# A state of 64 columns a head, and the inter part in 64 by 64 tiles, in a linear attention fused with a highway layer

## The chip, the core and the metric

The kernel runs on one core of a Trainium2 chip. The metric is the device time of one execution in microseconds. TensorE (PE) multiplies, VectorE (DVE), ScalarE (ACT) and GpSimd (POOL) do the elementwise work, and SyncE (SP) issues the transfers.

## What is computed

There are 4 sequences, 8 heads, 768 positions and 64 values a head. Attention is linear with a decay `lam` per head, done in blocks of 64 positions, with a 64 by 64 state carried from block to block:

```python
intra = np.einsum('bhic,bhjc->bhij', qb, kb) * Dmask[None]
intra = np.einsum('bhij,bhjd->bhid', intra, vb)
inter = np.einsum('bhid,bhde->bhie', qb * lam_pow[None], kv_state)
out[:, :, sl] = intra + inter
kv_state = lam_block[None, :, None, None] * kv_state + np.einsum('bhsd,bhse->bhde', kb_dec, vb)
...
x = np.ascontiguousarray(attn_out.transpose(0, 2, 1, 3)).reshape(B * S, H * D)
H = np.maximum(x @ w_h, 0.0)
T = 1.0 / (1.0 + np.exp(-(x @ w_t + b_t)))
return (T * H + (1.0 - T) * x).astype(np.float32)
```

The second part, a highway layer, takes the 3072 rows of 512 values that the attention gives.

## The kernel before

The work is cut into 12 chunks `n` of 256 positions, three to a sequence, and each chunk into two halves `b` of 128. The decay is moved into powers: `v` is weighed by `pow_v` when it is cast, the attention's result by `pow_o` when it leaves PSUM, so that the state only sums. The state is kept in one PSUM bank, `kv`, for the four pairs of heads `hp`; `e` is the head in its pair, and stands for the lower or upper 64 partitions.

For a chunk the kernel loads q, k and v, each in two transfers of 256 KB (`Lq`, `Lk`, `Lv`), casts them (`CQ`, `CK`, `CV`), turns q and k on PE (`RQF`, `RKF`, full 128 by 128 transposes, or `RQ`, `RK`, by 64 rows), evacuates them (`EQ`, `EK`, `FQ`, `FK`), multiplies scores (`S`, or `SA` and `SB` with state tiles between) and masks them on DVE (`M`), adds to the state (`U`) and copies the state out (`KE`, tile `ss`). The result `o` is a PSUM bank per half: `I` multiplies the inter part, `A` adds the intra part, and `D` brings it to `xT`. In `ss` a pair of heads is a 128 by 128 matrix, whose two blocks off the diagonal are zero, so `I` is one 128 by 128 matmul for a pair and a half:

```python
for hp in range(NP):
    T.matmul(get("o", n, b)[:, hp, :], lhsT=buf("ss", n, b)[:, hp, :], rhs=q_cols(n, slice(0, 128), hp, b),
             start=hp == 0, stop=False, skip_group_check=True)
```

The highway layer is done for each half of 128 rows, all 512 columns at a time. `TX` or `TXB` turns `xT` back to rows, which `XC` copies to `xs`; `BP` writes the bias into a bank, on which `F` with w=1 adds the four t matmuls, and `G` is the sigmoid; `F` with w=0 makes h in another bank. Then `H` takes max(h, 0) - x to `y` (DVE), `X` multiplies by the gate (POOL, sometimes DVE), `Y` adds x (POOL) and `ST` stores 512 KB. The last chunk goes another way in narrower pieces (`P`, `R`, `HX`, `YL`). The weights come in four transfers of 512 KB (`W`, 256 rows of w_h or w_t each) and are cast by `WC`. `Z` multiplies a blank tile to no use.

The order is written out by hand: `PLAN` is a list of such tokens, with the engine behind `@` and the PSUM banks behind `=`, and every engine works off its own part of the list in that order. All loads and stores go through one queue, SP's, and `UNDER_WAY` lets it issue a transfer only when the one eight places earlier has landed. Input buffers are rings of four chunks.

Of the kernel before, what the change touches and what calls it, by code (L numbers as in the profile page):

```python
# [21 lines left out]
WC.1.1.1@DVE Z.3=0 KE.1.0@ACT D.0.0@DVE Lv.2.1 WC.1.0.1@ACT WC.1.0.0@POOL M.1.0.1 U.1.1 TXB.0.0=0 BP.0.0.2@ACT=3
M.1.1.1 I.1=64 KE.1.1@ACT D.0.1@DVE F.0.0.1.2 Lk.3.1 WC.0.1.1@POOL WC.0.1.0@ACT M.1.0.0 BP.0.1.2@ACT=1 TXB.0.1=5 A.1.1
G.0.0.2 A.1.0 Lk.3.0 WC.0.0.1@DVE F.0.1.1.2 WC.0.0.0@ACT D.1.1@DVE XC.0.2.1@ACT Lq.3.1 F.0.1.0.2=2 D.1.0@DVE
XC.0.2.0@ACT Lq.3.0 G.0.1.2@S BP.1.1.2@DVE=4 TXB.1.1=5 F.0.0.0.2=0 H.0.1.2 Lk.5.1 CQ.2.2@ACT XC.1.2.1@DVE F.1.1.1.2
X.0.1.2@POOL H.0.0.2 Lv.3.1 CK.2.2@ACT BP.1.0.2@DVE=6 RQF.2=5 Lv.3.0 G.1.1.2@S Y.0.1.2@POOL TXB.1.0=1 X.0.0.2@DVE
RKF.2=2 XC.1.2.0@ACT F.1.1.0.2=0 EQ.2.1@DVE Lq.5.1 EK.2.0@ACT EK.2.1@DVE CV.2.2@POOL EQ.2.0@ACT S.2.1=14 Lk.4.1
H.1.1.2 F.1.0.1.2 M.2.0.1 Lk.5.0 CK.3.2@ACT S.2.0=25 M.2.1.1 X.1.1.2@POOL U.2.0 Lq.4.1 F.1.0.0.2=1 M.2.1.0 KE.2.0@ACT
Lq.4.0 CQ.3.2@ACT Y.0.0.2@POOL M.2.0.0 I.2=45 H.1.0.2 RKF.3=3 Lq.5.0 G.1.0.2@S A.2.1 Y.1.1.2@POOL EK.3.0@DVE
EK.3.1@ACT A.2.0 RQF.3=2 Lk.4.0 D.2.1@DVE X.1.0.2@POOL EQ.3.0@ACT D.2.0@DVE TXB.2.1=3 Lv.4.1 F.2.1.0.2=0  # L30
BP.2.1.2@ACT=1 EQ.3.1@DVE Lv.4.0 CV.3.2@POOL BP.2.0.2@DVE=6 XC.2.2.1@ACT TXB.2.0=2 F.2.1.1.2 H.2.1.2 XC.2.2.0@ACT
Lv.5.1 S.3.1=32 G.2.1.2@S S.3.0=54 Lq.6.1 Y.1.0.2@POOL M.3.0.1 U.3.0 CK.5.2@ACT F.2.0.0.2=0 Lq.6.0 M.3.1.0
X.2.1.2@POOL KE.3.0@ACT M.3.0.0 F.2.0.1.2 Lk.6.1 H.2.0.2 Lv.5.0 RKF.5=3 CQ.4.2@POOL G.2.0.2@S M.3.1.1 I.3=45 U.3.1
Lk.6.0 CK.4.2@ACT EK.5.1@DVE A.3.0 CQ.5.2@POOL A.3.1 EK.5.0@DVE RQF.4=2 D.3.0@DVE Lk.7.0 KE.3.1@ACT RKF.4=3
Y.2.1.2@POOL D.3.1@DVE BP.3.0.2@ACT=1 RQF.5=0 Lv.6.1 EQ.4.0@DVE EK.4.1@ACT TXB.3.0=6 TXB.3.1=4 EQ.5.0@DVE CV.4.2@POOL
F.3.1.0.2=5 EQ.5.1@ACT XC.3.2.0@DVE EK.4.0@DVE XC.3.2.1@ACT EQ.4.1@DVE S.5.0=60 H.3.1.2 F.3.0.1.2 CQ.6.2@ACT
X.2.0.2@POOL M.5.1.0 Lv.8.1 SA.4=3 M.5.0.0 Lv.6.0 S.4.1=42 BP.3.1.2@ACT=5 F.3.0.0.2=0 M.4.1.0 Y.2.0.2@POOL Lq.7.0
KE.4.0@ACT M.4.1.1 G.3.0.2@S F.3.1.1.2 Lk.8.1 CV.5.2@POOL H.3.0.2 CK.6.2@ACT SB.4=6 M.4.0.1 S.5.1=32 I.4=10 M.4.0.0
KE.4.1@ACT RKF.6=4 G.3.1.2@S M.5.0.1 X.3.0.2@POOL Lv.9.1 U.5.0 EK.6.0@ACT A.4.0 M.5.1.1 A.4.1 Lq.7.1 KE.5.0@ACT
RQF.6=6 X.3.1.2@POOL D.4.0@DVE EK.6.1@ACT Lq.8.0 I.5=32 EQ.6.1@DVE BP.4.0.2@ACT=5 TXB.4.0=1 Lq.9.1 D.4.1@DVE A.5.1  # L40
CV.6.2@POOL A.5.0 Lv.7.0 XC.4.2.0@DVE F.4.0.0.2=4 D.5.0@DVE Lk.7.1 D.5.1@DVE TXB.4.1=1 BP.5.0.2@ACT=0 Lk.8.0 TXB.5.0=3
F.4.0.1.2 Y.3.1.2@POOL H.4.0.2 XC.4.2.1@ACT Lv.7.1 XC.5.2.0@ACT BP.5.1.2@DVE=2 TXB.5.1=1 Lk.10.0 F.5.0.0.2=4 G.4.0.2@S
Y.3.0.2@POOL EQ.6.0@DVE Lv.8.0 XC.5.2.1@ACT BP.4.1.2@DVE=5 SA.6=3 Lq.9.0 X.4.0.2@POOL S.6.1=61 H.5.0.2 KE.6.0@ACT
F.5.0.1.2 Lk.9.1 M.6.1.0 CQ.7.2@POOL F.4.1.1.2 M.6.0.1 Lk.9.0 G.5.0.2 M.6.1.1 F.5.1.0.2=3 Y.4.0.2@POOL Lq.8.1
CK.7.2@ACT X.5.0.2@DVE F.4.1.0.2=6 H.5.1.2 G.4.1.2 CK.8.2@POOL Lk.11.0 RKF.7=1 Lk.10.1 H.4.1.2 SB.6=4 CV.7.2@POOL
EK.7.1@ACT RQF.7=0 EK.7.0@DVE KE.6.1@ACT M.6.0.0 I.6=13 RKF.8=6 EQ.7.1@ACT X.4.1.2@DVE A.6.0 EQ.7.0@ACT CV.8.2@POOL
EK.8.0@DVE A.6.1 Lv.11.0 EK.8.1@ACT S.7.1=45 D.6.1@DVE SA.7=0 Lq.11.1 CQ.9.2@ACT F.5.1.1.2 M.7.0.1 Lv.9.0 M.7.1.1
BP.6.1.2@ACT=3 TXB.6.1=6 Y.4.1.2@POOL F.6.1.0.2=4 Lv.10.0 XC.6.2.1@ACT M.7.1.0 Lv.10.1 KE.7.0@ACT F.6.1.1.2 D.6.0@DVE
CQ.8.2@POOL G.5.1.2@S Lq.10.0 H.6.1.2 CK.9.2@ACT TXB.6.0=5 Lq.11.0 SB.7=6 X.5.1.2@POOL XC.6.2.0@DVE RQF.8=0 M.7.0.0
KE.7.1@ACT I.7=51 Lv.11.1 EQ.8.1@DVE G.6.1.2@S Y.5.0.2@POOL RQF.9=6 CK.10.2@ACT A.7.1 Lq.10.1 EQ.9.1@DVE A.7.0  # L50
S.8.1=24 X.6.1.2@POOL Lk.11.1 D.7.1@DVE F.6.0.0.2=3 EQ.9.0@ACT EQ.8.0@ACT M.8.1.1 ST.3 CV.9.2@POOL F.7.1.0.2=6
BP.7.1.2@ACT=1 H.6.0.2 ST.2 D.7.0@DVE SA.8=0 BP.6.0.2@ACT=3 SB.8=4 M.8.1.0 F.7.1.1.2 KE.8.0@ACT ST.4 CV.10.2@POOL
BP.7.0.2@ACT=5 M.8.0.0 RKF.9=0 ST.0 G.7.1.2@S M.8.0.1 F.7.0.0.2=4 EK.9.0@ACT ST.1 EK.9.1@DVE TX.7.2=21 CQ.11.2@POOL
SA.9=0 XC.7.2.0@DVE F.7.0.1.2 XC.7.2.1@DVE KE.9.0@ACT Y.5.1.2@POOL M.9.1.0 CQ.10.2@ACT I.8=21 H.7.1.2 SB.9=0
CK.11.2@POOL ST.5 G.7.0.2@S H.7.0.2 A.8.1 A.8.0 KE.9.1@ACT RQF.11=6 D.8.1@DVE CV.11.2@POOL S.9.1=54 EQ.11.0@ACT
# [15 lines left out]

UNDER_WAY = 8

BUFS = dict(kf=4, qf=4, vf=4, kb=3, qb=2, vs=3, kT=2, qT=3, m=8, ss=4, xT=3, xs=3, y=6, ob=6, g=3)


@with_exitstack
def kernel(
# [13 lines left out]
    C = 128  # L92
# [404 lines left out]
```

## Time and profile before

| | |
|---|---|
| median of 3 runs | 105.09 us (105.09 to 105.13) |
| the profiled execution | 104.68 us, of which the span is 102.9 us |
| busy: PE, DVE, POOL, ACT | 92.4, 87.2, 78.9, 76.8 us |
| moved by transfers | 27.52 MB, mean 267 GB/s |
| mean granted clock of PE | 0.995 |

Times in the profile are microseconds from the start of the span. A group's row gives line, engine, operation, tiles, forms and count, then its busy time and the mean of one in ns, then the idle time ahead of it and what ended it. A row of the chain gives start, duration, engine, tile and line; a row of the table by stretch gives the stretch and its length, then the busy time of PE, weight loads, DVE, ACT and POOL with counts, the clock, the share of the transfer engines and GB/s. Busy times of PE hold pipelined latency, so the mean of one matmul is not its cost.

### The profile page before, as it was taken

What the parts mean: (1) busy time and instruction counts of PE and PEld (TensorE: products, weight loads), DVE (VectorE), ACT (ScalarE), POOL (GpSimd) and SP (SyncE); (2) the same over time, 40 slices, a digit from 0 to 9 for tenths busy, and PEclk for the clock granted to TensorE, in tenths of its full rate; (3) what the DMA queues carried; (4) which work ended last, traced back from release to release, by engine and by line L of the source; (5) the groups of instructions that cost most, each with busy time, mean ns of one, the idle gap of its engine ahead of it and who ended that gap; (6) DMA issues with size and microseconds to landing.
All of it is one profiled execution on the core that took longest, in us unless ns stands there. A gap on an engine that the chain in (4) does not pass through costs nothing.

```text
span 102.9 us, 4082 instructions
## 1 busy us (share of the span) xinstructions
PE 92.4 (90%) x1706; PEld 57.4 (56%) x1725; DVE 87.2 (85%) x164; ACT 76.8 (75%) x132; POOL 78.9 (77%) x78
## 2 busy tenths in 40 slices
PE   5997998899898999999999989999999899999900
PEld 1443565556376668458654865846745746555400
DVE  4237989599898799999999799797997999999960
ACT  3599974999968878989587679995996675584600
POOL 6704452406999999999989995999999969689540
PEclk9999999999999999999999999999999999999997
DMA  1999999999999999999999999999991361415243
GB/s 19 272 312 317 292 369 387 354 307 287 297 322 331 329 283 293 292 294 310 331 310 300 314 310 317 323 335 395 403 380 70 128 255 37 156 48 202 111 164 138
DMA packets 33479, 27.52 MB, mean 267 GB/s; under 512 B 1460, under 2 KB 26420, under 8 KB 33461
## 3 DMA queue, kind: packets, MB, share of 16 engines
q1 hardware_dynamic: 33456, 27.27, 87.4%
q8 instruction: 13, 0.21, 0.9%
q14 instruction: 6, 0.04, 0.1%
q10 hardware_dynamic: 4, 0.00, 0.0%
HBM read 20.97 MB, written 6.29 MB: 265 GB/s over the span
## 4 chain that ended last, share of the span: by engine, by line
PE 61%; ACT 10%; SPq 9%; DMA 8%; issue 4%; DVE 3%; POOLq 1%; POOL 1%; ACTq 0%
PE bt L386 17%; PE bh L386 16%; SPq L194 9%; DMA w_f<-in_moe_w_t_dram 8%; PE bs L273 5%; PE bo L343 5%; PE bo L334 4%; PE kv L278 3%; PE bktr L244 3%; PE bx L362 3%; PE bqtr L244 3%; ACT kT L113 2%; ACT w_b L113 2%; ACT g L404 2%; ACT xs L113 1%
## 5 line engine op out<-in xcount | busy, mean ns | idle before, releaser
L315 DVE TENSOR_TENSOR m<-bs,tri 128x512 bf16<-128x512 f32 x48 | 30.8, 682 | 0.9 <-PE bs L273 0.9
L386 PEld LDWEIGHTS <-xT 128*128 128x128 bf16 x200 | 17.1, 98 | 16.9 <-issue 0.4
L408 POOL TENSOR_TENSOR y<-g,y 128x512 bf16<-128x512 f32 x17 | 19.7, 1161 | 8.1 <-DVE y L399 6.0
L412 POOL TENSOR_TENSOR ob<-y,xs 128x512 f32<-128x512 bf16 x21 | 24.1, 1159 | 0.6 <-DVE y L408 0.3
L386 PE MATMUL bh<-w_b,xT 128*128 128x512 bf16 (+2 forms) x94 | 23.8, 362 | 0.6 <-issue 0.2
L232 POOL TENSOR_TENSOR vs<-vf,pow_v 128x1024 bf16<-128x1024 f32 (+1 forms) x12 | 21.9, 1835 | 3.0 <-DMA vf<-in_v_dram 2.9
L386 PE MATMUL bt<-w_b,xT 128*128 128x512 bf16 x89 | 23.3, 380 | 0.9 <-issue 0.8
L349 DVE TENSOR_TENSOR xT<-bo,pow_o 128x512 bf16<-128x512 f32 x24 | 15.9, 683 | 0.4 <-PE bo L343 0.3
L399 DVE SCALAR_TENSOR_TENSOR y<-bh,xs 128x512 bf16<-128x512 f32 x23 | 15.6, 685 | 0.6 <-PE bh L386 0.2
L404 ACT ACTIVATE g<-bt 128x512 f32<-128x512 f32 x18 | 10.8, 598 | 4.3 <-PE bt L386 4.2
L113 ACT ACTIVATE ss<-kv 128x512 bf16<-128x512 f32 x19 | 11.3, 593 | 3.5 <-PE kv L278 3.4
L273 PE MATMUL bs<-qT,kT 64*64 64x128 bf16 x384 | 11.7, 220 | 0.5 <-ACT qT L113 0.3
L113 ACT ACTIVATE bt<-b_bc 128x512 f32<-128x512 f32 x18 | 10.7, 601 | 1.6 <-DVE xT L349 1.0
L273 PEld LDWEIGHTS <-kT 64*64 64x64 bf16 x384 | 8.1, 106 | 3.2 <-DVE kT L115 1.1
L113 ACT ACTIVATE kb<-kf 128x1024 bf16<-128x1024 f32 x9 | 9.5, 1059 | 0.2 <-DMA kf<-in_k_dram 0.2
L278 PE MATMUL kv<-vs,kb 64*64 64x64 bf16 x320 | 8.9, 195 | 0.7 <-issue 0.7
L278 PEld LDWEIGHTS <-kb 64*64 64x64 bf16 x320 | 6.9, 109 | 3.9 <-issue 2.9
L113 ACT ACTIVATE xs<-bx 128x512 bf16<-128x512 bf16 x13 | 7.5, 593 | 1.2 <-PE bx L362 0.9
L343 PE MATMUL bo<-m,vs 64*64 64x128 bf16 x384 | 8.2, 218 | 0.2 <-DVE m L315 0.2
L113 ACT ACTIVATE kT<-bktr 128x512 bf16<-128x512 bf16 x10 | 6.0, 597 | 2.8 <-DVE kT L115 1.5
L115 POOL CAST qb<-qf 128x1024 bf16<-128x1024 f32 (+1 forms) x6 | 5.8, 972 | 2.8 <-DMA qf<-in_q_dram 2.8
L115 DVE COPY kT<-bktr 128x512 bf16<-128x512 bf16 x12 | 5.0, 421 | 3.4 <-PE bktr L244 2.1
(72 smaller groups left out, 135.2 us busy)
## 6 DMA issues: line engine op xcount, KB each, us to landing
qf<-in_q_dram SPq DMA_DIRECT2D x24, 256.0 KB, 5.1
kf<-in_k_dram SPq DMA_DIRECT2D x24, 256.0 KB, 5.4
vf<-in_v_dram SPq DMA_DIRECT2D x24, 256.0 KB, 5.4
out_dram<-ob SPq DMA_DIRECT2D x11, 512.0 KB, 4.9
w_f<-in_moe_w_t_dram SPq DMA_DIRECT2D x2, 512.0 KB, 6.8
w_f<-in_moe_w_h_dram SPq DMA_DIRECT2D x2, 512.0 KB, 9.5
out_dram<-ob SPq DMA_DIRECT2D x1, 256.0 KB, 2.0
out_dram<-ob SPq DMA_DIRECT2D x2, 64.0 KB, 1.6
```

The source lines that it names most:

```text
L113: A.activation(dst, src, AF.Copy)
L232: ENG[eng].tensor_tensor(buf("vs", n)[:, hs], in0=buf("vf", n)[:, hs].rearrange("p h (j d) -> p h j d", j=J), in1=pow_v[:, n % NST, hs, :, ...
L273: T.matmul(get("s", n, e, hp // 2)[half(b), hp % 2, j, :], lhsT=buf("kT", n)[half(e), hp, j, half(b)], rhs=q_cols(n, half(e), hp, b), star ...
L278: T.matmul(kv[half(e), hp, half(e)], lhsT=buf("kb", n)[half(b), j, 2 * hp + e, :], rhs=buf("vs", n)[half(b), 2 * hp + e, j, :], start=firs ...
L315: V.tensor_tensor(buf("m", n, e, u), in0=get("s", n, e, u), in1=tri[:, None].to_broadcast([128, 2, J, C]), op=ALU.mult)
L343: T.matmul(get("o", n, b)[half(e), hp, :], lhsT=buf("vs", n)[half(b), 2 * hp + e, j, :], rhs=buf("m", n, e, hp // 2)[half(b), hp % 2, j, : ...
L349: V.tensor_tensor(cut(buf("xT", n)[:, :, b * C:(b + 1) * C]), in0=get("o", n, b).rearrange("e k (j p) -> e k p j", j=Q), in1=cut(pow_o[:, ...
L386: T.matmul(t, lhsT=buf("xT", n)[:, j, b * C:(b + 1) * C], rhs=w_b[w][:, j, z], start=(j == 0 and not w), stop=(j == KC - 1), skip_group_ch ...
L399: V.scalar_tensor_tensor(buf("y", n, b)[:, z], in0=get("h", n, b, p), scalar=0.0, in1=buf("xs", n)[:, b, z], op0=ALU.max, op1=ALU.subtract)
L404: A.activation(buf("g", n, b)[:, cols(p)] if to == "S" else t, t, AF.Sigmoid)
L408: ENG[eng].tensor_tensor(y, in0=buf("g", n, b)[:, cols(p)] if eng == "POOL" else get("t", n, b, p), in1=y, op=ALU.mult)
L412: ENG[eng].tensor_tensor(buf("ob", n)[:, b, z], in0=buf("y", n, b)[:, z], in1=buf("xs", n)[:, b, z], op=ALU.add)
```

## The change

The state bank now holds 64 columns for a pair: head `e` of a pair lies in partition half `e`, and both heads share the columns. `ss` is half as wide. Two heads can no longer be one 128 by 128 matmul, so `I` multiplies 64 by 64 tiles, eight for a half of the chunk instead of four matmuls. Tiles that read the upper and the lower partitions may not write one bank together, so each of two groups pairs the lower head of one half `b` with the upper head of the other. For odd pairs of heads the result goes to the opposite partition half; `pow_o`, the weights' rows, `XC` and the transposes of `xT` (with a matrix `swap`) follow that order. Between the groups stands `RD`, a read of one column of the result's bank, for which the second group waits:

```diff
-    def inter(n, bk):
-        o_banks(n, bk)
-        for b in range(2):
-            if n % NST or b:
-                for hp in range(NP):
-                    T.matmul(get("o", n, b)[:, hp, :], lhsT=buf("ss", n, b)[:, hp, :], rhs=q_cols(n, slice(0, 128), hp, b),
-                             start=hp == 0, stop=False, skip_group_check=True)
-                begun.update((n, b, e) for e in range(2))
+    def inter(n, straight, bk):
+        if not straight:
+            o_banks(n, bk)
+        for u in range(2):
+            for e in range(2):
+                b = e if straight else 1 - e
+                if n % NST == 0 and b == 0:
+                    continue
+                for hp in (2 * u, 2 * u + 1):
+                    z = e ^ (hp % 2)
+                    i = T.matmul(get("o", n, b)[half(z), hp, :], lhsT=buf("ss", n, b)[half(e), hp, :], rhs=q_cols(n, half(e), hp, b),
+                                 start=o_first(n, b, z), stop=False, skip_group_check=True)
+                    if ("seen", n) in made:
+                        tc.add_manual_dep(i.ins, made.pop(("seen", n)), ...)
+    def order_rows(n, eng):
+        b = int(n % NST == 0)
+        made["seen", n] = read(eng, seen[half(b)], get("o", n, b)[half(b), 3, 0:1]).ins.name
```

The highway layer of chunks 0 and 1 (`COLUMNS`) is done by column halves: a block `F` takes both row halves and 256 columns, and the weights come by column halves in twelve transfers of 128 or 256 KB. `W.w.g.i` is matrix, column half and piece:

```diff
-    def load_w(w, g):
-        move(out=w_f[w][:, 2 * g:2 * g + 2],
-                          in_=(moe_w_h, moe_w_t)[w][256 * g:256 * g + 256].rearrange("(kc p) m -> p kc m", p=128))
+    def load_w(w, g, i):
+        z = slice(256 * g, 256 * g + 256)
+        w_in = (moe_w_h, moe_w_t)[w].rearrange("(j s p) m -> p j s m", s=4, p=64)[:, :, :, z]
+        if i == 0:
+            move(out=w_f[w][:, 0::2, z], in_=(moe_w_h, moe_w_t)[w].rearrange("(j s) m -> s j m", s=256)[0:128, :, z])
+        else:
+            move(out=w_f[w][half(i - 1), 1::2, z], in_=w_in[:, :, 4 - i])
```

Six units of 128 rows (2.1, 7.0, 9.1, 10.1, 10.0 and 11.0) take the gate another way, without `xs`, `X` and `Y`: `HP` is max(h, 0) times the gate, `RP` is (gate - 1) times x straight from the transposes' bank, and `Q` subtracts the second from the first:

```diff
+    def upper(n, b):
+        V.scalar_tensor_tensor(buf("ob", n)[:, b], in0=get("h", n, b, 2), scalar=0.0, in1=buf("g", n, b), op0=ALU.max, op1=ALU.mult)
+    def lower(n, b):
+        V.scalar_tensor_tensor(buf("r", n, b), in0=buf("g", n, b), scalar=1.0, in1=get("x", n, 2, b).rearrange("p k f -> p (k f)"),
+                               op0=ALU.subtract, op1=ALU.mult)
+    def merge(n, b, eng):
+        o = buf("ob", n)[:, b]
+        ENG[eng].tensor_tensor(o, in0=o, in1=buf("r", n, b), op=ALU.subtract)
```

`PLAN` is written anew. The 21 blank matmuls of `Z` become 16, the bias is written by ACT 23 times of 24, chunks 7 to 11 turn q and k by 64 rows instead of chunk 10 alone, and chunks 3, 4, 5 and 8 turn `xT` by 64 rows instead of 7, 8 and 9.

On SP, at the program's start, the loads stood like this before; `w_f1` is w_t, `w_f0` is w_h, and the digit behind `qf`, `kf`, `vf` is the chunk, with x2 for two transfers:

```order
L194 DMA vf1_130<-in_v_dram 128x4x128 x2
L194 DMA w_f1_118<-in_moe_w_t_dram 128x2x512 x2
L194 DMA w_f0_117<-in_moe_w_h_dram 128x2x512 x2
L194 DMA qf2_127<-in_q_dram 128x1x512
L194 DMA kf2_123<-in_k_dram 128x4x128
L194 DMA qf2_127<-in_q_dram 128x1x512
L194 DMA kf2_123<-in_k_dram 128x4x128
L194 DMA vf2_131<-in_v_dram 128x4x128 x2
L194 DMA kf3_124<-in_k_dram 128x4x128 x2
```

Now they stand like this from the same place on:

```order
L205 DMA vf1_133<-in_v_dram 128x4x128 x2
L205 DMA w_f0_120<-in_moe_w_h_dram 64x2x256
L205 DMA w_f1_121<-in_moe_w_t_dram 128x2x256
L205 DMA w_f1_121<-in_moe_w_t_dram 64x2x256 x2
L205 DMA w_f0_120<-in_moe_w_h_dram 64x2x256 x3
L205 DMA kf2_126<-in_k_dram 128x4x128
L205 DMA w_f0_120<-in_moe_w_h_dram 128x2x256
L205 DMA qf2_130<-in_q_dram 128x1x512 x2
L205 DMA w_f0_120<-in_moe_w_h_dram 128x2x256
L205 DMA kf2_126<-in_k_dram 128x4x128
L205 DMA vf2_134<-in_v_dram 128x4x128 x2
L205 DMA qf3_131<-in_q_dram 128x1x512 x2
```

Directly behind these stand the last three pieces of w_t and then chunk 3's k. So chunk 2's q has moved ahead of the last half of the weights, and the last of w_t behind chunk 3's q. In both orders 3072 KB are loaded by the end of the first row.

On DVE, where chunk 2's scores are masked (tiles `m`, from the banks `bs`), the queue was this before; `bh` is an h bank, `bktr` and `bqtr` are the banks of the transposes:

```order
L315 TENSOR_TENSOR m1_147<-bs_637,tri_93 128x512
L315 TENSOR_TENSOR m3_149<-bs_638,tri_93 128x512
L315 TENSOR_TENSOR m2_148<-bs_665,tri_93 128x512
L315 TENSOR_TENSOR m0_146<-bs_664,tri_93 128x512
L399 SCALAR_TENSOR_TENSOR y2_166<-bh_701,xs1_162 128x512
L115 COPY kT1_142<-bktr_723 128x512
L349 TENSOR_TENSOR xT2_160<-bo_713,pow_o_115 128x4x128
```

Now the read `RD` of chunk 2 stands between its masks:

```order
L331 TENSOR_TENSOR m3_152<-bs_682,tri_96 128x512
L331 TENSOR_TENSOR m2_151<-bs_700,tri_96 128x512
L331 TENSOR_TENSOR m0_149<-bs_727,tri_96 128x512
L113 COPY seen_185<-bo_753 64x1
L122 COPY qT0_146<-bqtr_737 128x16x32
L331 TENSOR_TENSOR m1_150<-bs_681,tri_96 128x512
L379 TENSOR_TENSOR xT2_163<-bo_753,pow_o_118 128x4x128
```

The read waits for PE, and three instructions that are independent of it stand behind it. Of the twelve reads seven are on DVE (chunks 2, 3, 5, 6, 7, 9, 11) and five on ACT (0, 1, 4, 8, 10).

On PE, at chunk 2's inter part, the order was a block of h, four matmuls of one half and four of the other, of which the last of the block, the first of a half and the start of the next half are shown:

```order
L386 MATMUL bh_701<-w_b0_119,xT1_159 128x512
L334 LDWEIGHTS ss0_154
L334 MATMUL bo_712<-qT2_145,ss0_154 128x128
...
L334 LDWEIGHTS ss1_155
L334 MATMUL bo_713<-qT2_145,ss1_155 128x128
```

Now the first group of eight tiles ends, the block of t of chunk 0 that takes the last column half of w_t stands between, and the second group follows:

```order
L356 LDWEIGHTS ss0_157
L356 MATMUL bo_753<-qT2_148,ss0_157 64x128
L432 LDWEIGHTS xT0_161
L432 MATMUL bt_667<-w_b1_123,xT0_161 128x256
...
L356 LDWEIGHTS ss1_158
L356 MATMUL bo_754<-qT2_148,ss1_158 64x128
```

The block's eight matmuls of 256 columns have taken the place between the two groups, and the second group now stands behind them and behind the read on DVE.

More of the change, by code (lines that the diff above doesn't have):

```diff
@@ L22 @@
[L22 to L31, printed above, removed]
@@ L318 @@
     begun = set()
+    seen = singles.tile([128, 1], F32)
     def o_first(n, b, e):
```

177 lines of the change are left out of this document (108 added, 69 removed).

## The prediction

> **What bounds the kernel now.** I read the page's busy times first, then the chain of waits, then the table by stretch for the part that the chain gives to TensorE, then the timeline of the start.
>
> ```profile
> PE 92.4 (90%) x1706; PEld 57.4 (56%) x1725; DVE 87.2 (85%) x164; ACT 76.8 (75%) x132; POOL 78.9 (77%) x78
> PE 61%; ACT 10%; SPq 9%; DMA 8%; issue 4%; DVE 3%; POOLq 1%; POOL 1%; ACTq 0%
> ...
> 10.31 7.78 DMA w_f<-in_moe_w_t_dram
> 18.11 0.63 ACT w_b L113
> ...
> 27.23 0.42 PE bs L273 x16
> ...
> 94.23 0.88 PE bt L386 x4
> ...
> 95.19 0.61 ACT g L404
> ...
> 99.17 0.69 DVE ob L412
> ```
>
> The chain has three parts. Up to 18.11 us it is transfers: their issue, then the 7.78 us of the t weights. Then ScalarE, which casts and evacuates for the first two chunks, up to 27.23. From there it is TensorE nearly without a break to 95.1, and a tail of sigmoid, gate and sum ends it. The stretch from chunk 2's first score to the last matmul:
>
> ```profile
> 27.20:97.70 70.50, 68.49 (x1388) 44.27 (x1404) 66.45 (x121) 54.52 (x94) 65.34 (x53) 1.00 0.87 266
> 97.10 0.60 PE L386 MATMUL bh<-w_b,xT 128*128 128x256 bf16 x4
> ```
>
> In these 70.50 us PE is busy 68.49, DVE 66.45 and POOL 65.34, ACT only 54.52; the granted clock is 1.00. So three engines are nearly full at once: a saving on PE alone ends soon at DVE. That is the main caution in what follows.
>
> **The change: matmul work.** Prices are the time that a run takes on the chain, by its count (the mean of one in a group holds latency too).
>
> ```profile
> 28.96 0.24 PE kv L278 x16
> 48.38 0.45 PE bo L334 x8
> 49.15 0.57 PE bo L343 x32
> 76.95 0.86 PE bh L386 x4
> 77.81 0.34 PE btr L260 x16
> ```
>
> So a 512-column block matmul costs 0.216 us, an inter matmul of 128 by 128 and 128 columns 56 ns (transposes are of that form), a 64 by 64 tile 18 ns, a state tile 15 ns, a transpose by 64 rows 21 ns. The 80 inter matmuls become 160 tiles of the form of the intra part: 80 x 56 = 4.5 us against 160 x 18 = 2.9. The four tiles of a group stand in different quadrants as intra's do; were there no overlap they would cost 56 each, so the bounds are 2.9 and 9.0, and I take 2.9, the row of the same form. Of the q and k transposes 64 full ones go and 128 by rows come: -3.6 + 2.7. For xT, 8 go and 16 come: -0.4 + 0.3. A block cut in column halves streams as many columns, priced the same. Over the kernel that is 2.6 us less.
>
> Switching tile mode has a price in this trace:
>
> ```profile
> 53.27 0.41 PE L273 MATMUL bs<-qT,kT 64*64 64x128 bf16 x16
> 53.84 1.67 PE L386 MATMUL bt<-w_b,xT 128*128 128x512 bf16 x7 [0.16 <-issue]
> ```
>
> After the 64 by 64 run PE idles 0.16 us. By the order, mode changes rise from 60 to 65 in all, but from the two markers below on there are 49 in each, so I add nothing there. The Trainium skill, "TensorEngine Tiling (Array Packing)", Key Properties, states that changing the tiling mode drains the array, which speaks against cutting inter in two; the gap of 0.16 agrees, and by it all five more would cost 0.8 us, which here fall in the start.
>
> **The change: when the dense part begins.** Weights now come in 12 pieces of 128 or 256 KB, spread among the loads of chunks 2 and 3. What counts is bytes: the last t piece is behind 7168 KB of loads, as chunk 3's k was before (28 of 256 KB, by the order of the queue); chunk 2's q is behind 5120 KB, as the last h weights were.
>
> ```profile
> 20.84 0.43 DVE L115 CAST w_b<-w_f 128x512 bf16<-128x512 f32 x1 [1.41 <-DMA w_f<-in_moe_w_h_dram]
> 27.41 1.06 ACT L113 ACTIVATE kb<-kf 128x1024 bf16<-128x1024 f32 x1 [0.20 <-DMA kf<-in_k_dram]
> 24.74 0.61 PE L244 MATMUL bqtr<-perm,qb 128*128 128x128 bf16 x8
> ```
>
> Both were waited for, so they landed at 20.84 and 27.41. Chunk 2's q transposes began at 24.74 before and can begin near 21.6 (20.84 and a cast). The block F of chunk 0 that takes the last t piece can begin at 27.41 plus a cast of 0.63 = 28.05. SP has 8 more issues; they hide behind its limit of eight transfers under way, and at most they make that block 2 us late, which I keep for the range. By then PE should have done six blocks, as before, and also chunk 2's scores, states and first inter group.
>
> Work left for PE by the prices above: before, from 27.23 on, 164 wide blocks 35.3, 184 transposes 10.3, 68 inter 3.8, 640 score and intra tiles 11.5, 256 state tiles 3.8, 80 row transposes 1.7, narrow blocks 0.9: 67.3 us, done in the 70.5 us to 97.70, a factor of 1.047. After, from that block on, 156 wide 33.6, narrow and half blocks 2.6, 104 transposes 5.8, 128 inter tiles 2.3, 608 tiles 10.9, 240 state 3.6, 224 row transposes 4.7: 63.5. Times 1.047 is 66.5; from 28.05 that ends at 94.55: **3.1 us earlier, by PE**.
>
> **The change: the other engines.** Six units (a chunk half of 128 rows) take another way through the highway sum: HP and RP on DVE and Q, in place of H, an xs copy, X and Y.
>
> ```profile
> L315 DVE TENSOR_TENSOR m<-bs,tri 128x512 bf16<-128x512 f32 x48 | 30.8, 682 | 0.9 <-PE bs L273 0.9
> L399 DVE SCALAR_TENSOR_TENSOR y<-bh,xs 128x512 bf16<-128x512 f32 x23 | 15.6, 685 | 0.6 <-PE bh L386 0.2 <-POOL ob L412 0.2 <-ACT xs L113 0.2
> L408 DVE TENSOR_TENSOR y<-bt,y 128x512 bf16<-128x512 f32 x6 | 4.1, 681 | 0.0
> L115 DVE COPY bt<-b_bc 128x512 f32<-128x512 f32 x6 | 4.1, 686 | 0.0
> L115 DVE COPY xs<-bx 128x512 bf16<-128x512 bf16 x11 | 4.4, 418 | 0.8 <-PE bx L371 0.8
> L113 ACT ACTIVATE ss<-kv 128x512 bf16<-128x512 f32 x19 | 11.3, 593 | 3.5 <-PE kv L278 3.4
> L412 POOL TENSOR_TENSOR ob<-y,xs 128x512 f32<-128x512 bf16 x21 | 24.1, 1159 | 0.6 <-DVE y L408 0.3
> L426 DVE TENSOR_TENSOR ob<-bh,ob 128x256 f32<-128x256 f32 x1 | 0.4, 415 | 0.0
> L145 DVE CAST tk_f<-tk_i 128x6 f32<-128x6 int32 x1 | 0.3, 297 | 0.5 <-POOL tk_i L135 0.5
> L124 DVE MEMSET ones<- 1x128 f32 x1 | 0.2, 165 | 0.0
> ```
>
> DVE loses 6 H, 6 X, 5 bias copies and 4 xs copies: 6 x 0.685 + 6 x 0.681 + 5 x 0.686 + 4 x 0.418 = 13.3 us. It gains 12 of HP and RP; no row reads f32 beside a bf16 PSUM tile, so RP lies between 0.418 and 0.685 and I take the upper: 8.2. It takes four more state evacuations, now of 256 columns (five of about 0.415 for one of 0.69: +1.4), one more bf16 copy (+0.4), and 7 reads RD of one column, between 0.165 and 0.297: 1.2 to 2.1; the wide copy of the bias, 0.7, moves to ACT. Net 1.4 to 2.1 us less. POOL's own count is 21 to 16 Y, five Q more, and fewer q casts: about 2 us less. ACT saves about 0.2 us on each of 15 state evacuations, takes 5 reads RD and more q casts, and stays the least loaded.
>
> So PE says 3.1 us and DVE, which was 94% full, at most 2.1, less the start it shares; these meet near 2.2. The tail is the same length within some tenths: the last sigmoid now stands 1.5 us further ahead of PE's last matmul, and RP, HP and the last four products fill that. The profiled execution took 104.68 (span 102.9), 0.41 under the median 105.09; from the median the forecast is 105.09 - 2.2 = **102.9 us**.
>
> **Rivals.** A: the forecast, its own range 101.9 to 103.9.
>
> B: the saving comes back as waits on DVE and POOL. Both are 93% full in the dense part; if they are filled no better than now, what stays is DVE's lower saving, 1.4, less the 0.8 us by which the new marker (28.05) stands behind the old (27.23): 104.5. For it speaks the table above, against it that each engine's own sum falls.
>
> C, on the other side: the turn of the row tiles. I.n.1 now waits for RD, which reads the bank of I.n.0 and stands in DVE's or ACT's queue; all PE work behind I.n.1 is held with it, and on DVE the masks behind RD. By the order, the PE work between the two groups is about 0.24 us in chunk 1, 0.86 in 2, 0.81 in 4, 0.68 in 5, 0.75 in 9, 0.60 in 11, and over 1.1 elsewhere. The round trip is a matmul's 0.22 (the latency in the group of intra), a read of about 0.23, and what stands ahead of it: one mask makes 1.13, and the shortfalls sum to 2.9 us, 105.8. With a further copy (0.42) ahead they sum to 6.4. A third of the way between is +4.1: 107.0. It decides when the wait takes 2.2 us over the 12 chunks, 0.18 each. The skill's same page, Gotcha 1, states that different row tiles may not use one PSUM bank at once and that software must see to it; no row here shows the case, since before inter had no row tiles.
>
> D: DVE is fed early enough to follow PE, so that PE's 3.1 us count in full, and half a microsecond goes from the tail: 105.09 - 3.6 = 101.5.
>
> E: the tiles do not overlap; 128 x (56 - 18) ns = 4.9 us more, 107.8. Intra in the same form speaks against it.
>
> **How the numbers follow.** A 0.45, D 0.10, B 0.15, C 0.27, E 0.03. Two tenths of a microsecond, 0.2%, is about what a measurement of this kernel can tell from no change. B reaches to no change for a third of it. Faster: 0.45 + 0.10 + 0.10 = 0.65; same 0.05; slower 0.30. The range reaches from half a microsecond under D to 106.5, where C's nearer half lies; what is left out is C's far half, E and a little under D, about 0.2.
>
> **What would show it.** Right: the chunk 2 q transposes near 21.6 us, the first block with the last t weights near 28.0, inter tiles under 0.2 us for eight on the chain, PE over 97% busy from there and its last matmul near 95. Wrong: PE's waits led by RD's copies on DVE or ACT (C), by masks or evacuations (B), PE idle for weight pieces past 28.5 us (the start term), or a tail over 5.5 us from the last matmul.

## The result, and the profile after

The changed kernel is slower: 110.72 us median against 105.11, and 1.037 times the time before, with a 95% interval of 1.031 to 1.042. (Some executions were disturbed, among them two of these four and the profiled ones of `w_rows` and `wide` below: medians here are of all executions, while ratios, on which the text rests, leave the disturbed ones out, so that of the changed kernel 108.95 and 109.42 count.) The forecast was 102.9, the range ended at 106.5. The profiled execution took 108.95 us, with a span of 107.2.

The page's first line, and the shares of the chain that ended last, which were 61% PE, 9% SPq and 8% DMA before:

```profile
PE 91.2 (85%) x1888; PEld 56.7 (53%) x1904; DVE 85.4 (80%) x166; ACT 76.0 (71%) x138; POOL 78.0 (73%) x78
PE 31%; DMA 23%; SPq 16%; DVE 8%; ACT 8%; issue 6%; POOL 3%; DVEq 0%; ACTq 0%; POOLq 0%
```

Every engine is busy for less time than before, as the sums had it, though PE and POOL save less than was summed: PE 1.2 us (2.6 by the prices, which leave latency out), DVE 1.8, ACT 0.8, POOL 0.9 (about 2). But 39% of the chain is now transfers and their issue, where it was 17%. Parts of it, the weights and the loads of the middle:

```profile
24.08 6.39 DMA w_f<-in_moe_w_t_dram
...
30.58 0.62 POOL w_b L122
...
31.24 1.03 PE bt L432 x8
32.27 0.24 PE bo L356 x8
...
43.06 7.23 DMA kf<-in_k_dram
...
60.48 1.05 POOL qb L122
...
63.41 5.19 DMA kf<-in_k_dram
...
68.71 0.65 ACT kb L120
```

The last t weights landed at 30.47 and the block that takes them began at 31.24, where 28.05 was forecast. The eight inter tiles behind it took 0.24 us, 30 ns each, which is little beside that. Then loads of k are waited for twice, at 43 and past 60 us; the chain of before has no load in those places. The first stretch by rate, before and after (stretch and length, busy times of PE, PEld, DVE, ACT, POOL, then clock, share of the transfer engines, GB/s); first before:

```profile
12.50:20.00 7.50, 6.65 (x148) 4.24 (x147) 6.59 (x12) 5.26 (x10) 3.02 (x3) 1.00 1.08 369
50.00:65.00 15.00, 14.48 (x261) 9.37 (x262) 14.35 (x26) 11.85 (x21) 13.40 (x12) 1.00 1.15 312
```

and the same two after, with the whole dense part behind them:

```profile
12.50:20.00 7.50, 6.55 (x181) 4.59 (x180) 6.54 (x13) 5.70 (x11) 3.43 (x3) 1.00 1.16 242
50.00:65.00 15.00, 13.59 (x338) 8.00 (x342) 12.72 (x26) 13.00 (x23) 11.84 (x10) 1.00 0.92 266
30.50:102.20 71.70, 66.28 (x1474) 40.53 (x1487) 64.08 (x121) 55.48 (x99) 62.20 (x49) 1.00 0.87 260
```

While the weights load, the transfer engines are as busy as before (1.16 against 1.08) and move a third less, 242 GB/s against 369. From 50 to 65 us they are not full (0.92, against 1.15), and PE idles 1.4 of 15 us where it idled 0.5. Those are two causes, and the experiments took them apart.

### The profile page after: what moved, and what is told of

Read it like the earlier page. It is cut to its first block, busy times and chain, and to the rows that moved or that the text cites. A ratio compares the mean times of both kernels' runs of the same rounds, so it can differ in the third digit from the quotient of the medians.

```text
span 107.2 us, 4459 instructions
## 1 busy us (share of the span) xinstructions
PE 91.2 (85%) x1888; PEld 56.7 (53%) x1904; DVE 85.4 (80%) x166; ACT 76.0 (71%) x138; POOL 78.0 (73%) x78
## 3 DMA queue, kind: packets, MB, share of 16 engines
q1 hardware_dynamic: 34608, 27.27, 89.3%
## 4 chain that ended last, share of the span: by engine, by line
PE 31%; DMA 23%; SPq 16%; DVE 8%; ACT 8%; issue 6%; POOL 3%; DVEq 0%; ACTq 0%; POOLq 0%
SPq L205 16%; DMA w_f<-in_moe_w_t_dram 12%; DMA kf<-in_k_dram 12%; PE bt L436 10%; PE bh L436 7%; PE bs L289 3%; PE bo L373 3%; ACT kb L120 3%; PE bo L356 2%; ACT qT L120 2%; DVE ob L462 2%; ACT kT L120 1%; PE kv L294 1%; DVE r L465 1%; DVE xT L379 1%
## 5 line engine op out<-in xcount | busy, mean ns | idle before, releaser
L436 PEld LDWEIGHTS <-xT 128*128 128x128 bf16 x168 | 14.4, 98 | 15.8 <-issue 2.5
L436 PE MATMUL bh<-w_b,xT 128*128 128x512 bf16 (+2 forms) x80 | 19.6, 359 | 2.1 <-issue 1.4
L436 PE MATMUL bt<-w_b,xT 128*128 128x512 bf16 x74 | 19.3, 380 | 0.5 <-issue 0.3
L459 POOL TENSOR_TENSOR ob<-y,xs 128x512 f32<-128x512 bf16 x16 | 18.2, 1159 | 0.1
L452 ACT ACTIVATE g<-bt 128x512 f32<-128x512 f32 x24 | 14.1, 592 | 3.6 <-PE bt L436 2.2
L120 ACT ACTIVATE bt<-b_bc 128x512 f32<-128x512 f32 x23 | 13.8, 605 | 3.9 <-DVE xT L379 3.8
L447 DVE SCALAR_TENSOR_TENSOR y<-bh,xs 128x512 bf16<-128x512 f32 x17 | 11.4, 683 | 0.3
L120 ACT ACTIVATE qb<-qf 128x1024 bf16<-128x1024 f32 x9 | 9.5, 1056 | 2.7 <-DMA qf<-in_q_dram 2.7
L120 ACT ACTIVATE kb<-kf 128x1024 bf16<-128x1024 f32 (+1 forms) x9 | 9.1, 1007 | 1.5 <-DMA kf<-in_k_dram 1.5
L356 PE MATMUL bo<-qT,ss 64*64 64x128 bf16 x160 | 7.4, 225 | 1.0 <-DVE seen L113 0.4
L432 PEld LDWEIGHTS <-xT 128*128 128x128 bf16 x64 | 6.0, 97 | 3.8 <-issue 2.9
```

Of the source, the lines that this page charges most:

```text
L120: A.activation(dst, src, AF.Copy)
L436: T.matmul(t, lhsT=buf("xT", n)[:, j, b * C:(b + 1) * C], rhs=w_b[w][:, j, z], start=(j == 0 and not w), stop=(j == KC - 1), skip_group_ch ...
L452: A.activation(part(buf("g", n, b), n, p) if to == "S" else t, t, AF.Sigmoid)
L459: ENG[eng].tensor_tensor(rows_of(buf("ob", n), n, b, p), in0=part(buf("y", n, b), n, p), in1=rows_of(buf("xs", n), n, b, p), op=ALU.add)
```

## The experiments

Ratios are to the kernel before, of runs on the same chip, with the 95% interval.

**Why the weights land late.** Five kernels have the order of before and only the weights' transfers changed. `w_cols` has the pieces of the change: column halves, 256 KB over 128 partitions for the even blocks of 128 rows and 128 KB over 64 partitions for the halves of the odd ones.

```diff
+        z = slice(256 * g, 256 * g + 256)
+        move(out=w_f[w][:, 0::2, z], in_=(moe_w_h, moe_w_t)[w].rearrange("(j s) m -> s j m", s=256)[0:128, :, z])
+        for e in range(2):
+            move(out=w_f[w][half(e), 1::2, z], in_=w_in[:, :, 2 + e])
```

> The kernel before, in its own order; only the weights come as in the changed kernel, by column halves in 128 or 256 KB pieces with runs of 1 KB, twelve transfers in place of four of 512 KB. Theory L (the weight pieces move slowly, and the loads behind them land late): GB/s from 12.5 to 20 us falls from about 370 to about 245, the last weights land 2 to 3 us later, and the time is 107 to 108.5. Rival O (the loads are only late because the new order is late): the rate stays above 340 and the time within 0.5 of 105.1.

108.09 us, 1.027 [1.021, 1.034]: the pieces alone cost most of what the change lost. `w_cols_full` keeps the column halves (rows of 1 KB) but takes each as one transfer of 512 KB over 128 partitions, and `w_rows` keeps the twelve pieces with their 64-partition halves, but in rows of 2 KB.

```diff
+        move(out=w_f[w][:, :, z], in_=(moe_w_h, moe_w_t)[w].rearrange("(kc p) m -> p kc m", p=128)[:, :, z])   # w_cols_full
...
+            move(out=w_f[w][half(e), 2 * g + 1], in_=w_in[r:r + 64])                                            # w_rows
```

> The kernel before; the weights come by column halves with runs of 1 KB, but in four transfers of 512 KB over all 128 partitions. If the run of 1 KB is what slows the pieces: as slow as with twelve pieces, about 107 to 108. If the size of the transfers or the 64 partitions is: 105.1, with about 370 GB/s from 12.5 to 20 us.

> The kernel before; the weights come in the same twelve sizes and partition halves as in the changed kernel (128 and 256 KB), but with runs of 2 KB. If the run is what matters: 105.1 and about 370 GB/s. If size or partition halves: about 107 to 108 and 245 GB/s.

`w_cols_full` 105.55 us, 1.0045 [1.001, 1.008]; `w_rows` 107.77, 1.025 [1.019, 1.031]. So it isn't the 1 KB rows. Left were the number and size of the transfers, and the 64 partitions. `w_half` has few transfers and large ones, but its odd blocks over 64 partitions (a matrix is one of 512 KB over 128 and two of 256 KB over 64); `w_small` has twelve small ones, all over 128.

```diff
+            move(out=w_f[w][half(e), 1::2], in_=w_in[:, :, 2 + e])          # w_half, 256 KB each
...
+            move(out=w_f[w][:, 2 * g + 1, z], in_=w_in[128:256, z])         # w_small, 128 KB each
```

> The kernel before; each weight matrix comes in one transfer of 512 KB over 128 partitions and two of 256 KB over 64 partitions each, runs of 2 KB. If the 64 partitions of a transfer are what slows it: between 105.1 and 107.8, near 106.5, with about 300 GB/s from 12.5 to 20 us, since half of the weight bytes go so. If the small size: 105.1 to 105.6, since no transfer is under 256 KB.

> The kernel before; the weights in twelve transfers of 256 and 128 KB as in the changed kernel, but every one over all 128 partitions, the small ones with runs of 1 KB. If the 64 partitions slow them: 105.1 to 105.6 and about 350 GB/s from 12.5 to 20 us. If the small size (fewer bytes under way at a limit of eight transfers): 107 to 108 and about 250 GB/s.

`w_half` 108.73 us, 1.024 [1.014, 1.033]; `w_small` 105.91, 1.006 [0.999, 1.012]. The rows of the same stretch, of `w_cols`:

```profile
12.50:20.00 7.50, 6.26 (x146) 4.07 (x143) 6.80 (x12) 3.54 (x6) 1.90 (x1) 1.00 1.14 253
```

of `w_cols_full`:

```profile
12.50:20.00 7.50, 7.10 (x153) 4.64 (x152) 7.08 (x13) 6.02 (x11) 3.12 (x3) 1.00 1.10 343
```

of `w_half`:

```profile
12.50:20.00 7.50, 5.98 (x171) 4.18 (x160) 5.97 (x11) 5.05 (x8) 2.51 (x2) 0.96 1.09 281
```

of `w_small`:

```profile
12.50:20.00 7.50, 7.50 (x186) 5.21 (x175) 7.00 (x13) 5.79 (x11) 3.13 (x3) 0.95 1.02 318
```

All three kernels with 64-partition transfers lose 2.4 to 2.7%, and the two whose rows stand here move 253 and 281 GB/s; both without lose 0.6% or less and move 343 and 318. The width in partitions is the cause, not the size, the count or the row length. That `w_half` loses as much as the twelve pieces, where half as much was expected, fits this too: in all three exactly half of the 2 MB of weights goes to 64 partitions at a time. One rival was not in the expectations: SP takes about 0.6 us to issue a piece in `w_cols`, and 0.33 to 0.43 us for most pieces in `w_small`. But `w_half` issues only two transfers more than before, SP stands waiting for its weight transfers to land, and it loses no less.

The Trainium skill, "SBUF — State Buffer", Door 1, states that a transfer to one half of the partitions reaches eight of sixteen ports; its table has 196 GB/s against 328 for a megabyte. The same page of the Trainium skill, "Can I just issue two DMAs to hit both halves?", adds that two transfers, one to each half, do not make up for it. The runs agree, with 253 and 281 GB/s against 318 and 343, though transfers to both halves were under way together.

**The compact state in the order of before.** `core` has the compact state, the tiles and `RD` at the places of `I` in the order of before, with the weights of `w_rows`; `core_full` loads the weights as before and exchanges the halves of the odd blocks when it casts them, with four casts more.

```diff
-I.2=45 H.1.0.2 RKF.3=3 Lq.5.0 G.1.0.2@S A.2.1
+I.2.0=45 RD.2@DVE H.1.0.2 RKF.3=3 Lq.5.0 G.1.0.2@S I.2.1 A.2.1                    # and so in every chunk
...
+            r = 128 + 64 * (1 - e)                                                  # core
+            move(out=w_f[w][half(e), 2 * g + 1], in_=w_in[r:r + 64])
...
+        for e in range(2):
+            copy(eng, w_b[w][half(e), 2 * g + 1], w_f[w][half(1 - e), 2 * g + 1])
```

> The compact state, the inter part in 64 by 64 tiles in two groups and the reads RD, in the order of the kernel before (the second group stands directly ahead of the first intra part); weights in twelve pieces with runs of 2 KB; no column halves, no other way through the gate. Theory L: the inter part itself is no cost: PE's inter tiles take under 0.2 us for eight, and the time stands within -1 to +1 us of the run with the same pieces in the kernel before. Rival C (the turn of the row tiles): 3 us or more slower than that run, with PE waiting for RD's copies.

> The compact state, the inter tiles and the reads RD in the order of the kernel before, as in the run core, but the weights in the four transfers of 512 KB of the kernel before; the casts of the odd weight blocks swap the partition halves instead (two casts of 64 partitions for one of 128, four more casts in all). Theory L (core was slow because of its weight transfers): about 2.7 us under core, 105.5 to 106.5. If the inter tiles save what the prices say and the turns cost nothing: 104 to 105. Rival C (the turns): 108 or more.

`core` 109.02 us, 1.041 [1.035, 1.047]; `core_full` 107.98, 1.021 [1.014, 1.028]. Neither came out as one of the expectations: `core` lies 1.7 us above `w_rows`, between the two that were named, and `core_full` between 106.5 and 108. The weights make the 2% between them. That `core_full` is still slower than before, though its inter tiles were priced lower, called for its parts one by one. `casts` is before with only the cut casts. `turn` is before with only the wait: `I` does two pairs of heads, `RD` reads that bank, and the other two pairs wait for it, at the places of `core_full`. `halves` cuts the 80 inter matmuls into 160 of 64 columns, for the number of instructions.

```diff
+                for hp in (2 * second, 2 * second + 1):
+                    i = T.matmul(get("o", n, b)[:, hp, :], lhsT=buf("ss", n, b)[:, hp, :], rhs=q_cols(n, slice(0, 128), hp, b), ...)
+                    if ("seen", n) in made:
+                        tc.add_manual_dep(i.ins, made.pop(("seen", n)), ...)
...
+            copy(eng, w_b[w][half(e), 2 * g + 1], w_f[w][half(e), 2 * g + 1])      # casts, for both e
...
+                    for c in range(2):                                              # halves
+                        T.matmul(get("o", n, b)[:, hp, 64 * c:64 * c + 64], lhsT=buf("ss", n, b)[:, hp, :],
+                                 rhs=q_cols(n, slice(0, 128), hp, b)[:, Q // 2 * c:Q // 2 * c + Q // 2], ...)
```

> The kernel before, with the four casts of odd weight blocks each done as two casts over 64 partitions (as in core_full, without the exchange of halves). If the casts make core_full's later start: four more of some 0.4 to 0.6 us, of which chunk 2's first score moves from 27.2 to about 28, and the time rises 0.6 to 1.0 us (+0.6 to +0.9%). If they hide beside the wait for the weights: within 0.3%.

> The kernel before, with only the turn: each chunk's inter part in two groups of pairs of heads, the second waiting for a read RD of the first's bank, in the places that core_full has them; matmuls, state and weights as before. If the turn makes core_full slow: +1.3 to +2.5 us (+1.2 to +2.4%), with PE's waits on the read over 1.5 us. If the tiles or the instruction count do: at most +0.5 us (+0.5%). The read itself costs 12 times 0.15 us beside other work.

> The kernel before, with each of the 80 inter matmuls cut into two of 64 columns: the same columns streamed, 80 matmul instructions more, nothing else. If the number of PE instructions matters (instruction queue beside full transfers): PE gaps without a waiting cause grow to over 1 us and the time rises 0.7 us or more. If it doesn't: the cost is that of streaming, 80 times 0 to 10 ns, and the time stays within +0.8 us, with no longer gap.

`casts` 105.75 us, 1.0033 [1.001, 1.006]; `turn` 107.76, 1.0245 [1.020, 1.029]; `halves` 106.06, 1.005 [1.002, 1.009]. The turn is nearly the whole of it. Who waits for the tile `seen` that `RD` writes, in `turn` (us in total, times):

```profile
L348 DVE COPY seen<-bo x7: 140/151/161, 30.4 to 92.4; 64x1 f32<-64x1 f32 x7
...
  PEld L337: 2.1, 5
  PE bo L337: 1.2, 4
```

The read takes 0.15 us; PE is stopped for 1.2 us by it, and its weight loads for 2.1. Chunk 2's first score is where it was (27.27 us, 27.23 before), and PE's last matmul ends 2.75 us later (100.45, 97.70). Beside the waits, the cut makes PE change its tile size 60 times from 20 us on, instead of 52; the gap that the prediction quoted, 0.16 us, would make 1.3 us of eight more. How the 2.75 us divide between the two wasn't tried. Turn and casts make 1.0279, if their costs simply add; `core_full` stands at 1.021, so the compact state and its tiles bring back about 0.7%, or 0.7 us (the intervals allow from nothing to 1.5%). No run shows where it comes from, and it does not seem to be PE's time: by its chain an inter tile of `core_full` takes 36 ns (129 in 4.59 us) and an intra tile 14 (350 in 4.99), against 57.5 for an inter matmul (64 in 3.68) and 17 (285 in 4.84) before, which makes an estimated 11.2 us for both parts against 11.1.

**The order of after.** `wide` is the changed kernel with the wide state and the 128 by 128 inter matmuls of before, and no `RD`; `wide_full` also loads each column half in one transfer over 128 partitions; `after_full` is the changed kernel with these transfers, exchanging halves in the casts; `after_full_q` loads q, k and v of chunks 5 to 11 in turn, where after sends some of the q of chunks 8 to 11 ahead, and has the last half of v behind four stores. The fourth piece shows the first of these places, the loads alone:

```diff
+    kv = ps.tile([128, NP, 128], F32, tag="kv", name="kv", bufs=1)                                              # wide
...
+        move(out=w_f[w][:, :, z], in_=(moe_w_h, moe_w_t)[w].rearrange("(kc p) m -> p kc m", p=128)[:, :, z])    # wide_full, after_full
...
+        copy(eng, w_b[w][:, 2 * i, z], w_f[w][:, 2 * i, z])                                                     # after_full
+        for e in range(2):
+            copy(eng, w_b[w][half(e), 2 * i + 1, z], w_f[w][half(1 - e), 2 * i + 1, z])
...
-Lq.5.1 Lq.5.0 Lk.5.1 Lq.8.1 Lk.5.0 Lq.6.1 Lv.5.0 Lv.5.1 Lq.6.0                                                  # after_full_q
+Lq.5.1 Lq.5.0 Lk.5.1 Lk.5.0 Lv.5.0 Lv.5.1 Lq.6.1 Lq.6.0
```

> The changed kernel in its own order, but with the state of 128 columns, the inter part as one 128 by 128 matmul for a pair and without the reads RD; all else, the weight pieces too, as changed. Theory L: the time stays near the changed kernel's, 108 to 111, with the weights as late, since the inter part is not what was lost. Rival C: 106 or less, as the wait of the second group is gone.

> The run before it (changed order, wide state), with each column half of a weight matrix in one transfer of 512 KB over 128 partitions, at the place of its first piece. Theory L: from 12.5 to 20 us about 350 GB/s, the block that takes the last t half begins near 28 us in place of 31, and the time is 3 us or more under that run. Rival O (the new order is slow by itself): within 1 us of that run.

> The changed kernel, but each column half of a weight matrix in one transfer of 512 KB over 128 partitions, with the same swapping casts. Theory L: 2 to 3 us under the changed kernel, 106.5 to 108, as the wide state showed with the same transfers; what is left over 105.1 then belongs to the order of the other loads and of the work. If the tiles are worth anything in this order, it is 0.5 to 1.5 under the run with the wide state.

> The run before it, with the loads of chunks 5 to 11 in the order in which the chunks take them (the changed kernel sends q of chunks 8, 9, 10 and 11 one to two chunks ahead, and SP then waits until the cast of four chunks earlier gives the buffer free, with k and v queued behind); the last v is also sent ahead of the stores. Theory Q (that wait is what is left): GB/s from 35 to 65 us rises from about 265 to about 300 and the time falls by 2 us or more, to 105 or under. Rival O (the order of the work, not of the loads): within 0.7 us of the run before it.

`wide` 110.27 us, 1.043 [1.034, 1.051]; `wide_full` 108.05, 1.023 [1.014, 1.032]; `after_full` 109.73, 1.036 [1.028, 1.045]; `after_full_q` 109.01, 1.022 [1.014, 1.030]. `wide` against the changed kernel (1.043 and 1.037) shows at once that the compact state, its tiles and the turn together are not what was lost. From `wide` to `wide_full` the transfers over 128 partitions are worth 2%, as in the order of before, or 2.1 us where 3 or more were expected. `after_full` was a miss: it seemed to say that in the whole change the transfers matter nothing. It had a cost of its own, its casts. There a cast of a column half becomes three (8 casts become 24, where `core_full` has four more), which the next runs measured. They all stand on `wide_full_q`, which is `wide_full` with the loads in turn. The turn is cut in as in `turn`, and the casts as in `after_full`, without the exchange:

> The kernel after_full_q (order of after, weights in 512 KB column halves over 128 partitions, q loaded in turn) with the wide state and 128 by 128 inter matmuls of before, no turn, uncut casts. If state, tiles, turn and their four casts cost in this order too (about what core_full lost): 1.0 to 2.0 us faster than after_full_q, 107 to 108 us, +1.5 to +2.5% less against before than after_full_q, so near +0.5 to +1.2%. If they cost nothing there (as wide against after): as after_full_q, +2.2%, and the rest is in the new order itself.

> wide_full_q with the turn alone: the inter part in two groups of pairs of heads, the second waiting for the read RD at the places where after has it; wide state, 128 by 128 matmuls, uncut casts. If the turn makes the loss in this order as it did in the order of before: +1.0 to +2.4% over wide_full_q, so 1.014 to 1.027 of before, with PE's waits on the read over 1.5 us. If the order of after hides it (in its trace PE waits on the read for only 0.9 us): +0 to +0.8%, so under 1.012.

> wide_full_q with the casts of the odd weight blocks cut into two casts over 64 partitions, as after_full_q has them. If the casts make the loss: +0.8 to +1.5%, so 1.011 to 1.019 of before. If they cost as in the order of before: +0.3%, so 1.004 to 1.010.

> wide_full_q with the turn and the cut casts. If these two are what the compact state costs: 1.018 to 1.026 of before, as after_full_q. If the tiles or the 80 more matmuls cost something of their own: 1.006 to 1.014, and the remainder to 1.022 is theirs. If the tiles save what they should (80 x 56 against 160 x 18 ns, 1.6 us, 1.5%): 1.03 or more.

`wide_full_q` 105.97 us, 1.0035 [1.000, 1.007]; with the turn alone (`wq_turn`) 106.73, 1.011 [1.006, 1.016]; with the cut casts alone (`wq_casts`) 108.61, 1.027 [1.021, 1.034]; with both (`wq_both`) 108.38, 1.029 [1.025, 1.033].

Loading in turn brings 1.9% from `wide_full` to `wide_full_q`, and 1.4% from `after_full` to `after_full_q`, where 2 us or more were expected; each has an uncertainty of about one percent. The middle of `wide_full`, which keeps the order of after:

```profile
50.00:65.00 15.00, 14.41 (x352) 8.57 (x354) 13.28 (x26) 13.38 (x24) 13.06 (x10) 1.00 0.95 264
```

and of `wide_full_q`:

```profile
50.00:65.00 15.00, 14.58 (x350) 8.81 (x348) 14.18 (x27) 13.80 (x25) 12.69 (x12) 1.00 1.10 308
```

The transfer engines are full again. In the order of after SP stands with a q load whose buffer isn't free, and k and v wait behind it, though theirs are. On SP's timeline of the changed kernel nothing is issued from 58.4 to 61.55 us:

```profile
55.50 2.87 SPq L205 DMA_DIRECT2D vf<-in_v_dram  x3
61.55 1.19 SPq L205 DMA_DIRECT2D qf<-in_q_dram  x2
```

What SP waits for is the cast of chunk 7's q at 60.48, in the chain above, which gives the buffer free for chunk 11's. A q load of chunk 9 and the two k loads of chunk 10 come next in the queue, and the k that ends this part of the chain lands at 68.60. Two earlier stops, from 37.10 to 38.84 and from 48.33 to 49.72 us, stand ahead of the first q loads of chunks 8 and 10 and end in the same way, right behind the cast of the q four chunks earlier.

The turn costs 0.7% here (from 0.1 to 1.3), a third of what it costs in the order of before; from `wq_casts` to `wq_both` it costs 0.1%, which can't be told from nothing. The waits on `seen` in `wq_turn`:

```profile
L359 DVE COPY seen<-bo x7: 136/151/163, 28.5 to 89.3; 64x1 f32<-64x1 f32 x7
...
  PEld L348: 0.5, 1
  PE bo L348: 0.4, 1
```

The order of after leaves enough PE work between `I.n.0` and `I.n.1`: one stop of 0.4 us instead of four. The changed kernel's own trace has the same two rows, 0.5 and 0.4. The changes of tile size are eight more here too, 58 from 20 us on against 50 in `wide_full_q`, so at 0.16 us each they would make more than the whole turn costs here.

The cut casts cost 2.4% (1.8% from `wq_turn` to `wq_both`), where 0.8 to 1.5 were expected. The weight casts of POOL in `wide_full_q` and then `wq_casts` (count, ns, shapes):

```profile
L119 POOL CAST w_b<-w_f x3: 611/614/616, 17.8 to 28.2; 128x512 bf16<-128x512 f32 x3
```

```profile
L119 POOL CAST w_b<-w_f x9: 394/398/407, 18.3 to 30.4; 64x256 bf16<-64x256 f32 x6, 128x256 bf16<-128x256 f32 x3
```

Half the partitions save nothing: 64 by 256 takes as long as 128 by 256, 0.40 us, so a column half costs 1.2 us instead of 0.62, and the first score of chunk 2 moves from 26.92 to 27.75. The last t block begins at 30.07 instead of 28.95, and behind its first matmul it stands 0.53 us for POOL's last cast, first `wide_full_q` and then `wq_casts`:

```profile
28.95 1.04 PE L411 MATMUL bt<-w_b,xT 128*128 128x256 bf16 x8
```

```profile
30.87 0.92 PE L413 MATMUL bt<-w_b,xT 128*128 128x256 bf16 x7 [0.53 <-POOL w_b L119]
```

So the block ends 1.8 us later, at 31.79, and the two profiled executions differ by as much. In the changed kernel the casts are whole, so this cost is only that of the experiments. `after_full_q`, which has turn, casts and tiles, stands 0.7% under `wq_both`; that would be the worth of the compact state and its tiles again, but the intervals overlap, so this pair alone doesn't show it.

So the parts of the change, from these runs, as shares of the time before: transfers over 64 partitions 2.0% (in the order of before 2.4 to 2.7), q out of turn 1.9%, the turn of the row tiles 0.7%, the compact state and its tiles -0.7%, all else in the new order and the new way through the highway sum 0.35%. They add to 4.3%; measured were 3.7% [3.1, 4.2], and each of them has an uncertainty of half a percent to one. No version beat the kernel before. Weights with exchanged halves in one transfer over 128 partitions, which would need neither the narrow transfers nor the cut casts, weren't tried.

## Why the prediction was wrong

**The start: the step that failed.** "What counts is bytes" put the last t weights behind 7168 KB, landing at 27.41 as chunk 3's k did. The bytes were counted right and the rate was taken as given. A megabyte of the weights went to 64 partitions, and at 242 GB/s instead of 369 they landed 3.06 us later, at 30.47. Of the 3.2 us by which the block that takes them was late, 2.3 went when they came over 128 partitions: it begins at 28.95 in `wide_full_q`. The page of the trace before had no such transfer. The bound beside it, "at most 2 us late", was given to SP's eight more issues, which was the wrong cause: `w_small` issues as many and loses 0.6%. This was named as a way to be wrong, "PE idle for weight pieces past 28.5 us", but it had no chance or price of its own, so the range ended too early.

**The loads in the middle: not in the prediction at all.** Only the start of SP's queue was read from the order. That q loads of later chunks stand ahead of k and v whose buffers are free sooner costs 1.4 to 1.9%, and it was there to be read.

**PE's and DVE's sums: DVE near, PE's tiles mis-sized, and the filling wrong.** DVE lost 1.8 us, inside the 1.4 to 2.1 that was said, but the terms listed there add to 1.9 to 2.8, so that it was luck in part. The tail is 5.1 us, 0.2 shorter than before, as said. The inter tiles were priced at 18 ns from runs of 32; on the chain of the changed kernel 84 of them take 2.42 us, 29 ns each, and the sign that was named, under 0.2 us for eight, did not come at the first of them. What stands ahead of them matters: eight took 0.24 us behind full matmuls, and 0.11 behind scores, which have the same tile size:

```profile
76.80 0.97 PE bt L436 x4
77.77 0.24 PE bo L356 x8
...
90.44 0.23 PE bs L289 x16
90.66 0.11 PE bo L356 x8
```

At 29 ns the 160 tiles take 4.6 us, as much as the 80 matmuls at 56 that they replace. In return the intra part, which now stands behind tiles of its own size, takes 14 ns a tile (192 in 2.77 us) instead of 17, about 1.0 us for all 384. By this estimate some 1.0 of the 1.6 us is left that the sum took from the inter part. And even with loads repaired and without tiles or turn, `wide_full_q` isn't faster than before:

```profile
28.90:98.70 69.80, 68.25 (x1424) 42.58 (x1421) 64.42 (x116) 56.48 (x95) 61.21 (x48) 1.00 0.88 263
```

From the block with the last t weights on, PE had 64.8 us of priced work there (the 63.5 of the prediction, and 1.3 more for wide inter matmuls), and took 69.8: a factor of 1.077, where 1.047 was taken from before. DVE is busy for 92% of it instead of 94. That is rival B's direction, a saving that comes back as idle time spread over many short waits; which of them, no run here tells.

**Rival C: the mechanism is real, its price depends on the order.** It was priced at 2.9 us or more in the order of after, from the PE work between the two groups and one mask ahead of the read. There it took 0.8 us by `wq_turn`, and less by `wq_both`, with one wait of PE of 0.4 us to be seen: in all chunks but one the read was done when PE came to the second group. In the order of before, with the groups closer together, it took 2.6. So the slower side of the forecast, 107.0 with 4.1 us for the turn, had the right sign for the wrong reason: what made the kernel slower is mainly the two causes above. **Rival E** fell: its price without overlap was 56 ns a tile, and the chain shows 29 on average.

## What to carry to other kernels

Before a transfer is split, look at how many partitions each piece covers: twelve pieces over 128 partitions cost 0.6% or nothing here, and pieces over 64 cost two and a half. In a queue that serves several rings of buffers in order, keep the loads in the order in which their buffers come free. A wait that is put between two groups of matmuls costs what the work between them doesn't cover, so its place in the order is worth more than the price of what is waited for: 2.4% in one order and 0.7% or less in the other. A price that was read from a long run of tiles doesn't hold for a short one behind another tile size: 29 ns here, not 18.

## What the runs showed of the hardware that was not expected

The 64-partition transfers: 242 to 281 GB/s in a stretch that has 318 to 369 without them, at transfer engines that are just as busy (1.09 to 1.16 against 1.02 to 1.10).

PE stops in the middle of a block, with all it needs at hand. The longest is in `after_full_q`, between the second and third matmul of a block:

```profile
72.61 0.60 PE L433 MATMUL bh<-w_b,xT 128*128 128x512 bf16 x2 [2.09 <-issue]
```

The page counts 13 to 15 packets of 16 KB on a queue of kind "instruction" (q8), three to fourteen microseconds apart. In the twenty kernels' traces there are eleven stops of PE of 0.4 us or more for which nothing is waited (one of 0.7 in before, 2.09 the longest), and every one ended 1.3 to 1.8 us after one of these packets was through; the packet ahead of the 2.09 us took 2.11 us instead of about 1.1. With packets so far apart, eleven of eleven in half a microsecond is not chance. That PE runs out of instructions when such a packet comes late would fit, but it is not shown: the packets ahead of other stops took no longer than usual (0.94 us ahead of one of 1.02), and no run was made that moves these packets. The changed kernel's profiled execution has two such stops, of 0.88 and 0.53 us; what they add to its time is open. The number of matmuls is not what made the change slow: `halves`, with 80 more and one stop of 0.60, loses 0.5%, and `turn` and `wide_full_q` have no such stop.
